# Expert 0 of a fused retention and mixture-of-experts kernel: a joint second layer for 96 early and 224 late places, and a new order of the preparation around it

## The chip, the cores and the metric

The kernel runs on one core of one Trainium2 chip. The metric is the device time of one execution in microseconds (us). The kernel before takes 393.67 us in the median of three runs (392.56, 393.67 and 394.03).

## What is computed

The reference is a retention layer (a linear attention with a decay per head) followed by a mixture of eight experts, in which every token goes to one expert alone:

```python
for t in range(S):                       # B=4, H=8, S=768, D=64
    state = gamma * state + k_t^T v_t
    y[t] = scale * q_t @ state
x = y as (3072 tokens, 512)
logits = x @ w_gate; expert_idx = argmax(logits)
gate_w = softmax(logits)[expert_idx]
for e in range(8):                       # w1: 512 x 1024, w2: 1024 x 512
    h = np.maximum(x[mask_e] @ w1[e], 0)
    out[mask_e] = gate_w[mask_e] * (h @ w2[e])
```

Counted from the reference's own inputs (its seed is 0), expert 0 gets 185 tokens of the first 1536 and 174 of the last 1536; the other seven get 347 to 417.

## The kernel before

**The attention part** works on 24 chunks of 128 tokens, two to a step, k = 0 to 11. A step multiplies scores, carries the state, forms the outputs, turns the tokens' rows (`rows`, L299), computes the gate's logits (`logits` L315, its copy to `LT` at L320, `finish_logits` L322) and, for groups of chunks, ranks the tokens (`gating`, L336). Each chunk's rows are sent to a table in HBM, sorted by expert, by an indirect DMA that GpSimd issues (`send_x`, L306; `SENDS` says which chunks in which step). `after` (L446) holds GpSimd's queue until a value is there.

**Expert 0 is done in two parts.** Its tokens of the first twelve chunks ("early", at most `EARLY` = 224 places) are worked on while the last chunks are still being gated: `early_half` (L698) computes their hidden layer (`hidden`, in halves handed out by `FILL`, with the low parts by `low`) and their output rows (`result`, L722, and `send`, L736). Its other tokens ("late", `CAPS[0]` = 224 places) are position 0 of `moe_main` (L744). The seven other experts follow, sorted by their counts, with `CAPS[1:]` places.

**Precision.** Every product is made of three float32r products of high and low parts: weights are cast on ScalarE into `whi` and the rest subtracted into `wlo` (`split`, L136; 512 or 1024 columns at a time), tokens likewise into `xh` and `xl`, hidden values into `hh` (ScalarE, L897) and `hl` (VectorE, L898). A part of the weights is 1 MB, four parts to an expert; `fetch` (L129) brings one into one of two `raw` buffers, on SyncE's queue. The split weights and other tiles share 11 slots in a pool.

**The first layer** of a position has 8 steps f, each with 12 matmuls into one of three PSUM tiles `ph`, over the position's whole width. **The second layer** has two forms. "Natural" (`natural`, positions 0 and 7): the hidden values are stationary, 128 tokens at a time, the weights move, 24 matmuls of 512 columns for each 128 tokens, and the rows are scaled (`put_rows`, L816) and scattered whole. The other form: a quarter of the weights' columns is stationary, the tokens move, 24 matmuls over the whole width for each of four quarters k; the result in one of two PSUM tiles `py` is transposed on VectorE into `Z` (`turn`, L827), weighted (`weigh`, L833) and scattered in slices of 128 values by GpSimd (`put_slices`, L838), 32 places at a time, during the next position.

**Four widths.** `by_count` (L779) branches on TensorE over four copies of the matmuls: `CAPS[e]`, or 1, 2 or 3 `STEPS` less, by the number that `count_columns` (L776) loads into a register. Position 0 has one width.

**The order is written out by hand** (`manual_schedule`): `jobs` in `moe_main` (L851 to L879) hang the splits, fetches and weightings on the steps f and k. At position 0 the next expert's rows are prepared (`prep_x`, L810: a transpose on VectorE, a cast on ScalarE, a subtraction) at k = 0, three of the four blocks with the subtraction on GpSimd. Parts 0 and 1 of expert 1 are split at f = 2, 3, 5, 6, part 2 at k = 0. In the attention part `SPLITS` (L55) says at which step two quarters of a part of expert 0 are split.

## Time and profile before

| | |
|---|---|
| time, median of three runs | 393.67 us (392.56 to 394.03) |
| the profiled execution: its time, and the span of its instructions | 394.31 us, 392.5 us |
| TensorE (PE) busy | 381.1 us (97% of the span), 3277 matmuls |
| its weight loads (PEld) busy | 354.2 us (90%) |
| VectorE (DVE) busy | 246.6 us (63%) |
| ScalarE (ACT), GpSimd (POOL) busy | 153.4 us (39%), 165.1 us (42%) |
| the chain that ended last, by engine | PE 83%, DMA 7%, issue 4%, DVE 2% |
| granted TensorE clock | 0.997 |

A row of a timeline gives start, duration, engine, line, operation, the names of what is written and read, the shape, and in brackets the idle time of the engine before it with what ended that. PE is TensorE, PEld its weight loads, DVE VectorE, ACT ScalarE, POOL GpSimd, SPq the DMA queue of SyncE. A row of the chain gives start, duration and what ran, with the count of instructions. Attention takes the span up to about 103 us, mixed with the start of expert 0; the rest is experts.

### The profile page before, as it was taken

How to read it: one execution, taken by the hardware profiler on the slowest of the kernel's cores; microseconds unless marked ns; L12 is line 12 of the kernel's file. 1: busy time of each engine (PE TensorE's matmuls, PEld its weight loads, DVE VectorE, ACT ScalarE, POOL GpSimd, SP SyncE). 2: the span in 40 equal slices, each digit the busy share in tenths (PEclk: the TensorE clock that was granted, in tenths of full speed). 3: DMA queues.
4: the chain of work that ended last, by engine and by line, in shares of the span. 5: the costliest groups of instructions: out<-in, count | busy, mean ns of one | idle time of the engine just before them, and what ended most of it. 6: DMA issues, size and time to landing. Idle time of an engine off the chain costs nothing.

```text
span 392.5 us, 8600 instructions
## 1 busy us (share of the span) xinstructions
PE 381.1 (97%) x3277; PEld 354.2 (90%) x3277; DVE 246.6 (63%) x475; ACT 153.4 (39%) x308; POOL 165.1 (42%) x153
## 2 busy tenths in 40 slices
PE   7998999999899999999999999999999999999993
PEld 4787889888798979999999999999999999999972
DVE  4548756795795766773966387477738657666220
ACT  2335435553641545531552354054334415423100
POOL 0333646676751040000485078218506822841552
PEclk9999999999999999999999999999999999999998
DMA  7998899997348778375356557825844773530111
GB/s 276 404 359 315 319 410 384 383 362 253 131 134 236 245 200 254 132 186 143 130 161 202 142 175 244 210 97 168 230 136 152 253 187 137 179 123 10 43 56 50
DMA packets 29821, 80.57 MB, mean 205 GB/s; under 512 B 4556, under 2 KB 18384, under 8 KB 23348
## 3 DMA queue, kind: packets, MB, share of 16 engines
q1 hardware_dynamic: 24740, 66.80, 52.2%
q0 software_dynamic: 5008, 12.69, 8.7%
q8 instruction: 58, 0.95, 1.0%
q14 instruction: 15, 0.12, 0.1%
HBM read 65.00 MB, written 15.08 MB: 204 GB/s over the span
## 4 chain that ended last, share of the span: by engine, by line
PE 83%; DMA 7%; issue 4%; DVE 2%; SPq 2%; POOL 1%; ACT 0%; POOLq 0%; DVEq 0%
PE ph L888 33%; PE py L922 27%; PE py L920 6%; PE Y L287 3%; DMA qkv_t<-qkv 3%; DMA raw<-w 3%; PE sp L246 3%; PE py L729 3%; PE ph L712 3%; PE xp L302 2%; PE U L260 2%; PE Y L276 1%; DMA xn<-xs_dram 1%; PE L L318 1%; SPq L225 1%
## 5 line engine op out<-in xcount | busy, mean ns | idle before, releaser
L670 POOL DMA_INDIRECT out<-Z,sidx x80 | 93.9, 1173 | 136.8 <-DVE Z L836 99.9
L142 DVE TENSOR_TENSOR wlo<-raw,whi 128x1024 fp32r<-128x1024 f32 (+1 forms) x66 | 76.6, 1164 | 12.1 <-ACT whi L141 11.2
L141 ACT CAST whi<-raw 128x1024 fp32r<-128x1024 f32 (+1 forms) x72 | 67.5, 951 | 4.0 <-DMA raw<-w 3.9
L897 ACT ACTIVATE hh<-ph 128x224 fp32r<-128x224 f32 (+7 forms) x64 | 31.2, 489 | 94.5 <-PE ph L888 81.8
L922 PE MATMUL py<-hh,whi 128*128 128x392 f32 (+4 forms) x192 | 66.0, 344 | 0.0
L922 PE MATMUL py<-hl,whi 128*128 128x392 f32 (+4 forms) x192 | 65.9, 343 | 0.0
L922 PE MATMUL py<-hh,wlo 128*128 128x392 f32 (+4 forms) x192 | 65.7, 342 | 0.0
L898 DVE SCALAR_TENSOR_TENSOR hl<-ph,hh 128x224 fp32r<-128x224 f32 (+7 forms) x64 | 35.2, 551 | 35.0 <-ACT hh L897 30.2
L888 PE MATMUL ph<-xh,wlo 128*128 128x392 f32 (+5 forms) x224 | 49.1, 341 | 0.0
L888 PE MATMUL ph<-xh,whi 128*128 128x392 f32 (+5 forms) x224 | 48.9, 340 | 0.0
L888 PE MATMUL ph<-xl,whi 128*128 128x392 f32 (+5 forms) x224 | 48.8, 339 | 0.0
L888 PEld LDWEIGHTS ph<-xl,whi 128*128 128x128 f32 x224 | 40.3, 188 | 0.2
L888 PEld LDWEIGHTS ph<-xh,whi 128*128 128x128 f32 x224 | 40.2, 188 | 0.3
L888 PEld LDWEIGHTS ph<-xh,wlo 128*128 128x128 f32 x224 | 40.3, 188 | 0.2
L689 ACT CAST xh<-xt 128x512 fp32r<-128x512 f32 (+7 forms) x26 | 14.4, 555 | 57.4 <-DVE xt L680 52.0
L922 PEld LDWEIGHTS py<-hh,wlo 128*128 128x128 f32 x192 | 36.1, 188 | 0.2
L922 PEld LDWEIGHTS py<-hl,whi 128*128 128x128 f32 x192 | 36.0, 188 | 0.2
L922 PEld LDWEIGHTS py<-hh,whi 128*128 128x128 f32 x192 | 36.0, 188 | 0.1
L235 POOL TENSOR_TENSOR vs<-qkv_t,cs 128x512 f32<-128x512 f32 x19 | 19.8, 1041 | 38.1 <-DMA qkv_t<-qkv 31.0
L249 DVE TENSOR_TENSOR Sb<-sp,xgs 128x512 f32<-128x512 f32 x48 | 29.8, 682 | 4.4 <-PE sp L246 4.4
L831 DVE STREAM_TRANSPOSE Z<-py 128x416 f32<-128x416 f32 (+3 forms) x24 | 15.0, 626 | 24.6 <-PE py L922 22.9
L265 ACT ACTIVATE ub<-U,cs 128x64 f32<-128x64 f32 x80 | 18.6, 315 | 26.1 <-PE U L260 25.7
(141 smaller groups left out, 523.1 us busy)
## 6 DMA issues: line engine op xcount, KB each, us to landing
raw<-w SPq DMA_DIRECT2D x32, 1024.0 KB
qkv_t<-qkv SPq DMA_DIRECT2D x18, 1024.0 KB
qkv_t<-qkv SPq DMA_DIRECT2D x4, 768.0 KB
xgs<-xs_dram SPq DMA_DIRECT2D x12, 211.2 KB
qkv_t<-qkv SPq DMA_DIRECT2D x4, 512.0 KB
xgs<-xs_dram SPq DMA_DIRECT2D x8, 195.0 KB
out<-Z,sidx POOLq DMA_INDIRECT x80
xs_dram<-zero SPq DMA_DIRECT2D x6, 195.0 KB
```

Of the source, the lines that this page charges most:

```text
L141: nc.scalar.copy(out=hi[:, h], in_=raw[:, h])
L142: engine.tensor_tensor(out=lo[:, h], in0=raw[:, h], in1=hi[:, h].bitcast(F32), op=ALU.subtract)
L235: engine.tensor_tensor(out=vs, in0=qs[g][:, 2].rearrange("a (h d) -> a h d", d=D), in1=cv[:, c, :].unsqueeze(2).broadcast_to([P, H, D]), o ...
L249: nc.vector.tensor_tensor(out=Sb[:, r], in0=sps[r], in1=M[:, r], op=ALU.mult)
L265: nc.scalar.activation(out=ubs[g % 3][:, p], in_=U[:, p], func=AF.Copy, scale=k_("ratio")[:, at:at + 1])
L670: sc = tc.nc.gpsimd.indirect_dma_start(out=out, out_offset=bass.IndirectOffsetOnAxis(ap=index, axis=0), in_=rows, in_offset=None, bounds_c ...
L831: nc.vector.transpose(out=Zs[e][:, 0:nb, k, :], in_=py[:, 0:32 * nb].rearrange("p (j c) -> p j c", c=32))
L888: nc.tensor.matmul(out=ph[:, :w], lhsT=wparts[e, f // 4][a][:, kd, fo:fo + P], rhs=x[:, kd, :w], start=(n == 0), stop=(n == 3 * KD - 1))
L897: nc.scalar.activation(out=hh[:, :cap], in_=ph[:, :cap], func=AF.Relu)
L898: nc.vector.scalar_tensor_tensor(out=hl[:, :cap], in0=ph[:, :cap], scalar=0.0, in1=hh[:, :cap].bitcast(F32), op0=ALU.max, op1=ALU.subtract)
L920: nc.tensor.matmul(out=py[:w, :], lhsT=x[:, k * P:k * P + w], rhs=a[:, f % 4, :], **se)
L922: nc.tensor.matmul(out=py[:, :cols], lhsT=a[:, f % 4, k * P:(k + 1) * P], rhs=x[:, :cols], **se)
```

## The change

- **Expert 0's second layer.** Only the first 128 early tokens keep their own second layer (`result(0, ..)`, `send(0)`). The other 96 early places (`REST`) and the 224 late ones get a joint one in the form of experts 1 to 6: four quarters k, 24 matmuls each, in four widths of 320, 304, 288 or 272 columns, 16 apart (`WIDE`, `STEPS`), chosen by the late count. `hh` and `hl` become one ring of 9 each, and the 96 early places are copied into it at f = 1. Ten slices of 32 places are transposed, weighted and scattered; their names and weights are taken by `take_names`.
- **Expert 1's preparation.** Splits: part 0 at f = 2, 3; part 1 at k = 1, 2; part 2 at k = 3. `prep_x` goes to f = 7, k = 0 (two) and k = 1, with the subtraction on VectorE. The fetch of part 3 moves from f = 7 to k = 2.
- **Before position 0.** The rows of the late tokens are prepared ahead of the counts and limits on VectorE; the clearing behind expert 1's rows is issued before its weights.
- **In attention.** `SPLITS` moves a pair of quarters from step 3 to 4 and one from 4 to 5; `SENDS` moves one chunk from step 11 to 10; `FILL` moves half a hidden step behind the last ranking; one `low` goes from GpSimd to VectorE.

```diff
-STEPS = [0, 10, 8, 8, 8, 8, 8, 8]
+REST = EARLY - 128
+WIDE = [REST + EARLY, *CAPS[1:]]
+STEPS = [16, 10, 8, 8, 8, 8, 8, 8]
-FILL = (1, 3, 2, 2)
+FILL = (1, 2, 3, 2)
-SENDS = {4: (0, 1), 5: (1, 3), 6: (3, 5), 7: (5, 7), 8: (7, 10), 9: (10, 12), 10: (12, 15), 11: (15, 18)}
-SPLITS = {3: (0, 1), 4: (2, 3), 7: (4, 5), 8: (6, 7), 9: (8, 9), 10: (10, 11)}
+SENDS = {4: (0, 1), 5: (1, 3), 6: (3, 5), 7: (5, 7), 8: (7, 10), 9: (10, 12), 10: (12, 16), 11: (16, 18)}
+SPLITS = {4: (0, 1), 5: (2, 3), 7: (4, 5), 8: (6, 7), 9: (8, 9), 10: (10, 11)}
...
-        for i, g in enumerate(range(SENDS[NCH // 2 - 1][1], GROUPS[-1][0])):
+        for g in range(SENDS[NCH // 2 - 1][1], GROUPS[-1][0]):
             send_x(g)
-            if i == 1:
-                lows(1, nc.gpsimd)
...
-        load_meta(meta8, E, 2)
+        end_of = lambda i: nc.sync.value_load(end7[0:1, i - 1:i], min_val=0, max_val=(E9 + 1) * N)
+        clear(bass.ds(end_of(1), ZROWS))
         number = lambda i: nc.sync.value_load(eid7[0:1, i - 1:i], min_val=1, max_val=E - 1)
         expert_at[1] = number(1)
         fetch(1, 0)
-        end_of = ...
-        clear(bass.ds(end_of(1), ZROWS))
...
+        lows(KF, nc.vector)
+        token_index(sidx0, meta0, cnt0)
+        xhl1 = new_xhl()
+        ... (turn_slices and cut_slices of xt1, moved up here)
         (limit, fits, spare, far, beyond)
-        lows(KF, nc.vector)
-        token_index(sidx0, meta0, cnt0)
         result(0, 0)
         result(0, 1)
         send(0)
-        ... (turn_slices and cut_slices of xt1)
-        result(1, 0)
-        result(1, 1)
-        send(1)
+        take_names(late_from, xg1)
+        ... (gone0, slices0)
...
             if more:
-                for part, s0, f0 in ((0, 3, 0), (1, 6, 2)) if e else ((0, 2, 4), (1, 5, 7)):
-                    job(f0, fetch, e + 1, part if e else part + 2)
+                if not e:
+                    for i, eng in halves:
+                        job(2 + i, split, 1, 0, i, eng)
+                        job(KF + 1 + i, split, 1, 1, i, eng)
+                        job(KF + 3, split, 1, 2, i, eng)
+                    job(4, fetch, 1, 2)
+                    job(KF + 2, fetch, 1, 3)
+                    for j, f in enumerate((KF - 1, KF, KF, KF + 1)[:nxt]):
+                        job(f, prep_x, 1, j, nc.vector)
...
-                if e == 0 and f < 3:
-                    nc.vector.memset(ph[:, cap:], 0.0)
                 (hh on ScalarE, hl on VectorE)
+                if e == 0 and f < 3:
+                    nc.vector.memset(ph[:, cap:], 0.0)
+                if e == 0 and f == 1:
+                    early = [h[:, :, P:EARLY].bitcast(F32) for h in hhl0]
+                    nc.scalar.copy(out=HH[:, 0:KF, 0:REST], in_=early[0])
+                    nc.vector.tensor_copy(out=HL[:, 0:KF, 0:REST], in_=early[1])
+                if e == 0 and f in (3, 4):
+                    nc.vector.memset(pys[f - 3][:, WIDE[0] - 3 * STEPS[0]:CMAX32], 0.0)
...
-                    prep_x(e + 1, j, nc.gpsimd if not e and j < 3 else nc.vector)
-                if not e and k == 0:
-                    for i, eng in halves:
-                        split(1, 2, i, eng)
+                    prep_x(e + 1, j, nc.vector)
+                for fn, a in jobs[KF + k] if not e else ():
+                    fn(*a)
```

How the order moves is shown at three places. The first is ScalarE from attention step 3 to step 5: `whi` is a cast of expert 0's weights, `xgs<-L` the copy of the logits to `LT`, `xn<-xp` the tokens' rows, `ub` belongs to the state, `ex` to the gate of step 3. Before:

```order
L265 ACTIVATE ub_119<-U,cs 128x64 x4
L141 CAST whi<-raw 128x512 x2
L320 COPY xgs<-L 128x256
L304 COPY xn<-xp 128x4x128 x2
L265 ACTIVATE ub_120<-U,cs 128x64 x4
L364 ACTIVATE ex<-sh 128x48
L265 ACTIVATE ub_121<-U,cs 128x64 x4
L141 CAST whi<-raw 128x512 x2
L320 COPY xgs<-L 128x256
```

After:

```order
L271 ACTIVATE ub_120<-U,cs 128x64 x4
L326 COPY xgs<-L 128x256
L310 COPY xn<-xp 128x4x128 x2
L271 ACTIVATE ub_121<-U,cs 128x64 x4
L370 ACTIVATE ex<-sh 128x48
L271 ACTIVATE ub_122<-U,cs 128x64 x4
L144 CAST whi<-raw 128x512 x2
L326 COPY xgs<-L 128x256
L310 COPY xn<-xp 128x4x128 x2
L271 ACTIVATE ub_120<-U,cs 128x64 x4
L271 ACTIVATE ub_121<-U,cs 128x64 x4
L144 CAST whi<-raw 128x512 x2
```

In step 3 no cast stands ahead of the copy of the logits any more; steps 4 and 5 have one each.

The second place is VectorE from the last counts to the first `hl` of position 0. `xt` and `xhl` are the late tokens' rows, `xn<-py` the scaled early rows, `limit` to `beyond` the limits. Before:

```order
L621 TENSOR_SCALAR beyond<-far 128x105
L720 TENSOR_TENSOR hl_1618<-rx_1616,hh_1617 128x224 x2
L190 TENSOR_SCALAR far<-cs,cnt_78 128x2
L192 TENSOR_SCALAR ids<-meta_82 128x2
L194 SCALAR_TENSOR_TENSOR sidx_84<-ids,far 128x2
L733 TENSOR_SCALAR xn<-py_2046,meta_82 128x4x4x32
L680 STREAM_TRANSPOSE xt_1827<-xg_1826 128x4x4x32
```

In the changed kernel, after the last subtraction of the late rows:

```order
L703 TENSOR_TENSOR xhl<-xt_1830,xhl 128x4x32
L629 TENSOR_TENSOR se<-sel,cnt 128x49
L630 TENSOR_REDUCE limit<-se 128x7
L631 TENSOR_TENSOR limit<-limit,cs 128x7
L634 TENSOR_TENSOR fits<-cnt,cs 128x3
L635 TENSOR_TENSOR fits<-limit,cs 128x3x7
L638 TENSOR_REDUCE spare<-fits 128x8
L640 TENSOR_TENSOR far<-cs,limit 128x105
L642 TENSOR_SCALAR beyond<-far 128x105
L746 TENSOR_SCALAR xn<-py_2059,meta_82 128x4x4x32
L413 TENSOR_SCALAR slices_84<-xg_1829 128x7
L415 COPY share_86<-xg_1829 128x7
```

The limits stood ahead of the late rows and now stand behind them; behind these rows come three more small instructions (`gone` twice, `slices`) and then the first `hl`.

The third place is VectorE in position 0's second layer: `xt`, `xl` belong to expert 1's rows, `wlo` to its weights, `yo` and `Z` to position 0's results. Before:

```order
L680 STREAM_TRANSPOSE xt<-xgs 128x4x4x32 x3
L680 STREAM_TRANSPOSE xt<-xgs 128x3x4x32
L690 TENSOR_TENSOR xl<-xt,xh 128x4x68
L142 TENSOR_TENSOR wlo<-raw,whi 128x1024 x2
L822 TENSOR_SCALAR yo<-py_2148,meta_83 128x4x4x32
```

After:

```order
L703 TENSOR_TENSOR xl<-xt,xh 128x4x128
L693 STREAM_TRANSPOSE xt<-xgs 128x4x4x32
L703 TENSOR_TENSOR xl<-xt,xh 128x4x128
L842 STREAM_TRANSPOSE Z<-py_2122 128x10x32
L145 TENSOR_TENSOR wlo<-raw,whi 128x1024
L794 UNCONDITIONAL_BRANCH
L693 STREAM_TRANSPOSE xt<-xgs 128x3x4x32
L703 TENSOR_TENSOR xl<-xt,xh 128x4x68
L842 STREAM_TRANSPOSE Z<-py_2123 128x10x32
L794 UNCONDITIONAL_BRANCH x4
L145 TENSOR_TENSOR wlo<-raw,whi 128x1024
L842 STREAM_TRANSPOSE Z<-py_2122 128x10x32
```

Three blocks of expert 1's rows now stand ahead of the first transpose into `Z`, the fourth and a split ahead of the second.

More of the change, by code (lines that the diff above doesn't have):

```diff
@@ L500, in retention_moe @@
             if last:
-                hidden, low, result, send = early_half(tc, ring[:, 4:6].rearrange("a j q m -> a j (q m)")[:, :, 0:DM],
+                hidden, low, result, send, hhl0 = early_half(tc, ring[:, 4:5].rearrange("a j q m -> a j (q m)")[:, :, 0:DM],
                                             wk.tile([P, 4, EARLY], F32, name="rx0", tag="xT"),
@@ L581, in retention_moe @@
             nc.vector.tensor_reduce(out=eid7, in_=se, axis=AX.X, op=ALU.add)
-        for i in (14, 15):
-            split(0, *divmod(i, 4), nc.vector, 1)
         past = gsm.tile([P, E1], F32, name="past")
@@ L626, in retention_moe @@
         send(0)
-        xhl1 = new_xhl()
-        pieces = ((0, P), (4, 64), (6, EARLY - P - 64))
-        for j, w in pieces:
-            turn_slices(nc, xt1, xg1, j, w)
-        for j, w in pieces:
-            cut_slices(nc, nc.vector, xhl1[:, 0], xhl1[:, 1], xt1, j, w)
-        result(1, 0)
-        result(1, 1)
-        send(1)
-        token_index(sidx8, meta8, cnt[:, E:E + 1])
+        take_names(late_from, xg1)
+        for at, first, n, lim in ((0, NJ0 - late_from, late_from, cnt0), (late_from, 0, NJ0, cnt[:, E:E9])):
+            nc.vector.tensor_scalar(out=gone0[:, at:at + n], in0=k_("slot")[:, first:first + n], scalar1=lim,
+                                    scalar2=float(BIG), op0=ALU.is_ge, op1=ALU.mult)
+        nc.vector.tensor_tensor(out=slices0, in0=slices0, in1=gone0, op=ALU.add)
     def overflow():
@@ L651, in clear_behind @@
         nc.sync.dma_start(out=x_rows[bass.ds(end_at[e], ZROWS), :], in_=zero)
-    natural = {0: (sidx8, meta8)}
-    moe_main(tc, wparts, fetch, split, xhl1, xgs, clear_behind, load_x, load_meta, token_index, regions, beyond, limit, spare, natural,
-             overflow, out)
+    moe_main(tc, wparts, fetch, split, xhl1, hhl0, slices0, share0, xgs, clear_behind, load_x, load_meta, token_index,
+             regions, beyond, limit, spare, overflow, out)
     most = nc.values_load(top[0:1, 0:1], min_val=0, max_val=N)
@@ L738, in send, with moe_main @@
         scatter_rows(tc, out, sidx0[:w, j:j + 1], yo[:w, j, :])
-    return hidden, low, result, send
+    return hidden, low, result, send, (hh, hl)
 @with_exitstack
-def moe_main(ctx, tc, wparts, fetch, split, xhl1, xgs, clear_behind, load_x, load_meta, token_index, regions, beyond, limit, spare, natural,
-             overflow, out):
+def moe_main(ctx, tc, wparts, fetch, split, xhl1, hhl0, slices0, share0, xgs, clear_behind, load_x, load_meta, token_index,
+             regions, beyond, limit, spare, overflow, out):
     nc = tc.nc
@@ L758, in moe_main @@
     widths = [[min(P, c - a) for a in range(0, c, P)] for c in CAPS]
-    blocks = [-(-c // 32) for c in CAPS]
+    blocks = [-(-c // 32) for c in WIDE]
     xs = {0: (xhl1[:, 0], xhl1[:, 1])}
@@ L873, in moe_main @@
             if more:
-                for part, s0, f0 in ((0, 3, 0), (1, 6, 2)) if e else ((0, 2, 4), (1, 5, 7)):
-                    job(f0, fetch, e + 1, part if e else part + 2)
+                if not e:
[7 more added lines that the diff above has]
+                        job(f, prep_x, 1, j, nc.vector)
+                for part, s0, f0 in ((0, 3, 0), (1, 6, 2)) if e else ():
+                    job(f0, fetch, e + 1, part)
                     for i, eng in halves:
@@ L939, in moe_main @@
                     fetch(e + 1, 3)
[L940 removed]
+                for fn, a in jobs[KF + k] if e else ():
                     fn(*a)
```

86 lines of the change are left out of this document (53 added, 33 removed).

## The prediction

> **What bounds the kernel now.** I read the stretches first (engines busy in a piece of the span), then the chain that ended last. The columns of a stretch are its bounds and length, the busy time of PE, PEld, DVE, ACT and POOL with their instructions, clock, DMA share and GB/s:
>
> ```profile
> 91.60:96.90 5.30, 5.30 (x94) 4.43 (x94) 3.20 (x7) 1.30 (x5) 2.48 (x5) 1.00 0.71 211
> ...
> 112.60:118.30 5.70, 5.70 (x28) 4.62 (x27) 4.39 (x18) 0.81 (x3) 1.73 (x4) 1.00 0.52 101
> ...
> 134.50:145.70 11.20, 11.20 (x51) 8.45 (x51) 8.47 (x12) 4.97 (x8) 3.84 (x3) 1.00 0.71 222
> 145.70:182.50 36.80, 36.80 (x194) 36.10 (x193) 22.99 (x38) 14.10 (x20) 1.92 (x2) 1.00 0.70 199
> 182.50:381.00 198.50, 198.50 (x1106) 195.94 (x1105) 124.28 (x198) 73.58 (x108) 93.87 (x80) 1.00 0.49 150
> ```
>
> In each of the stretches from 112.6 on TensorE is busy for the whole length, and the chain, which names its matmuls by stage (start, length, count), has no gap in between. So a matmul taken out after 112.6 is worth its full time, unless the change makes TensorE wait:
>
> ```profile
> 91.68 0.34 SPq L177
> ...
> 92.58 3.62 DMA xn<-xs_dram
> ...
> 112.86 11.12 PE py L729 x48
> 123.98 10.71 PE ph L888 x96
> 134.69 11.13 PE py L920 x48
> 145.83 18.40 PE ph L888 x96
> 164.23 18.40 PE py L922 x96
> ...
> 271.22 17.20 PE py L922 x96
> ```
>
> The first two rows are the load of expert 0's early rows; the next three are expert 0: early output rows (two blocks, 512 columns), late first layer (224 columns), late output rows (two blocks, 512). Expert 1 follows (422 columns); the last row is expert 5's second layer (392 columns).
>
> **The matmuls.** Removed are 24 of the 48 of L729 and all 48 of L920: 11.12/2 + 11.13 = 16.69 us. Added are 4 x 24 = 96. The late count is 174 (counted from the reference's inputs), not above 224 - 3 x 16 = 176, so the branch takes 272 columns. No row has 272. The nearest on both sides are 224 columns, 10.71/96 = 0.1116 us each, and 392, 17.20/96 = 0.1792 us; on the line between them 272 columns cost 0.1116 + 48 x 0.000402 = 0.1309 us. So the 96 take 12.57 us and the change saves **4.12 us**. Bounds: all as cheap as at 224 columns gives 5.97; the widest of the four (320 columns, 0.1502 us) gives 2.27.
>
> The Trainium skill ("TensorE: Matmul & The Clock Gate", section "Wait — 56ns, not 53.3ns?") gives columns divided by 2.4 GHz plus about 2.5 ns. By it 512 columns cost 0.2158 us where the trace has 0.2317, and the saving would be an estimated 4.4 us; the trace decides.
>
> **What TensorE may newly wait for.** First, position 0 now starts when the first early block is done (118.4 on this trace's scale), 5.56 us sooner, and its rows must be there. The rows that make them, and what stands around them on VectorE:
>
> ```profile
> 113.09 2.02 SPq L177 DMA_DIRECT2D xg<-xs_dram  x4
> 114.88 0.21 DVE L610 TENSOR_TENSOR se<-sel,cnt 128x49 f32<-128x49 f32 x1
> 116.18 0.22 DVE L621 TENSOR_SCALAR beyond<-far 128x105 int32<-128x105 f32 x1
> 118.47 0.75 DVE L733 TENSOR_SCALAR xn<-py,meta 128x512 f32<-128x512 f32 x1 [1.07 <-PE py L729]
> 119.14 1.22 DVE L680 STREAM_TRANSPOSE xt<-xg 128x512 f32<-128x512 f32 x3
> 119.88 1.13 ACT L689 CAST xhl<-xt 128x512 fp32r<-128x512 f32 x3 [6.15 <-DVE xt L680]
> 120.60 1.23 DVE L690 TENSOR_TENSOR xhl<-xt,xhl 128x512 fp32r<-128x512 f32 x3 [0.24 <-ACT xhl L689]
> ...
> L898 DVE SCALAR_TENSOR_TENSOR hl<-ph,hh 128x224 fp32r<-128x224 f32 x8 | 3.0, 386 | 1.3 <-ACT hh L897 0.8 <-issue 0.4
> L894 DVE MEMSET ph<- 128x228 f32 x3 | 0.7, 248 | 0.7 <-PE ph L888 0.6 <-issue 0.2
> ```
>
> From the first transpose to the last cast is 119.88 + 1.13 - 119.14 = 1.87 us, to the last subtraction 2.69. Ahead of them VectorE loses the limits (114.88 to 116.40), so it reaches them near 115.8. When their load landed, no row says; the load of the early rows, of the same size, took from 91.68 to 92.58 + 3.62 = 96.20, 4.52 us, at a DMA share of 0.71. From 113.09 that would be 117.6. Here the share is 0.52, and the last sends, behind which the load waits, lose a `low` of GpSimd ahead of them; I take 115.8 and keep 117.6 as the bound. The rows are then cast by 117.7 and subtracted by 118.5: in time.
>
> Behind them VectorE has the limits (1.5 us and one small instruction more, 1.75), the scaled rows (0.75) and five small ones near 0.2: the first `hl` runs at 122.0 to 122.4, the clearing of its bank to 122.65. TensorE wants that bank again at the fourth step, 118.4 + 3 x 10.71/8 = 122.4: a wait of **0.2**. Then come `hl` and a clearing for two more banks and the copy of 768 early columns (no row shows it; between 0.4 and 0.9, as 1024 columns subtract in 1.22 below); the fifth and sixth steps find their banks free. With the load at 117.6 TensorE would start 1.1 late and wait 0.9 at the fourth step.
>
> Second, expert 1's rows stand ahead of the first transpose that frees a result bank. One block's work shows in expert 1's own second layer:
>
> ```profile
> 166.93 0.70 DVE L680 STREAM_TRANSPOSE xt<-xgs 128x512 f32<-128x512 f32 x1
> 168.32 0.69 DVE L690 TENSOR_TENSOR xl<-xt,xh 128x512 fp32r<-128x512 f32 x1 [0.69 <-ACT xh L689]
> 168.93 0.68 DVE L831 STREAM_TRANSPOSE Z<-py 128x480 f32<-128x480 f32 x1
> ...
> L142 DVE TENSOR_TENSOR wlo<-raw,whi 128x1024 fp32r<-128x1024 f32 x18 | 21.9, 1220 | 3.6 <-ACT whi L141 3.6
> ```
>
> A block takes 168.93 - 166.93 = 2.0 us, since VectorE waits for the cast in the middle. On the old scale the first layer ends at 129.3, the last `hl` 0.9 later; three blocks end at 136.2, the transpose of 320 columns (0.5, from 0.68 for 480) at 136.7. TensorE has done k = 0 and 1 at 129.3 + 2 x 3.14 = 135.6 and wants that bank: a wait of **1.1**. The second transpose comes after a split (1.2) and the short block (1.5), at 139.9, when k = 2 ends: nothing more. Expert 1 starts near 143.0 instead of 145.8, and its rows are ready at 139.4. Bounds: 0 if VectorE gets through the blocks faster, 2.5 if it comes a microsecond later.
>
> Third, weights. The fetch of expert 1's last part now waits on SyncE for a split that VectorE makes at 141.0; queued behind it on SyncE are the clearing, expert 2's rows and its weights. Their rows before, and the one cast that shows a landing behind such rows:
>
> ```profile
> 122.47 1.94 SPq L177 DMA_DIRECT2D xgs<-xs_dram  x4
> ...
> 137.25 0.37 SPq L651 DMA_DIRECT2D xs_dram<-zero  x1
> 142.71 1.91 SPq L177 DMA_DIRECT2D xgs<-xs_dram  x4
> 145.21 0.35 SPq L133 DMA_DIRECT2D raw<-w  x1
> ...
> 132.82 1.05 ACT L141 CAST whi<-raw 128x1024 fp32r<-128x1024 f32 x1 [0.41 <-DMA raw<-w]
> ```
>
> From clearing to rows is 5.46 us, from rows to the cast of the weights behind them 132.82 - 122.47 = 10.35. So expert 2's first weights land at 141.4 + 5.5 + 10.35 = 157.2, while ScalarE asks for them after expert 1's fourth step, 143.0 + 4 x 18.40/8 + 0.7 = 152.9. ScalarE stands still meanwhile, and the hidden values of the fifth step behind it come at 158.3, their low part at 159.4; TensorE wants that bank at the eighth step, 143.0 + 7 x 2.30 = 159.1: **0.3**, between 0 and 2. The ten scatters and three weightings added to expert 1's time lie beside its matmuls: POOL is busy 1.92 of 36.8 us there, DVE 22.99.
>
> **Attention.** In step 3 a cast of weights stands in ScalarE's queue ahead of the copy of the logits:
>
> ```profile
> 33.73 1.14 ACT L141 CAST whi<-raw 128x512 fp32r<-128x512 f32 x2 [2.79 <-DMA raw<-w]
> 34.78 0.36 ACT L320 COPY xgs<-L 128x256 f32<-128x256 f32 x1
> 35.19 0.44 PE L328 MATMUL lp<-cs,xgs 128*128 128x128 f32 x2 [1.06 <-ACT xgs L320]
> ```
>
> The cast waits 2.79 us for its DMA, the logits' copy behind it is late, TensorE stands 1.06 us. With the pair moved the weights are there before step 4. I take **1.1 us**, carried through to the end of attention because all that feeds the end of attention starts from there; bounds 0 (the later loads from HBM don't come sooner) and 1.5 (the subtraction that leaves step 3 delays other work too). One send of a chunk (128 rows of 520 words, 266 KB) now falls into the load of the early rows that starts at 91.6; the stretch moves 211 GB/s, so it costs between 0 and 1.26. I take **0.4**: the stretch's DMA is busy 0.71 only.
>
> The rest costs nothing: `FILL` only exchanges matmuls that TensorE does anyway, the splits of steps 4 and 5 find their weights landed, and the clearing that goes ahead of expert 1's weights on SyncE delays them by its own 0.37 us, 5 us before they are split.
>
> **Sum.** -1.1 + 0.4 - 4.1 + 0.2 + 1.1 + 0.3 = -3.2. The profiled execution, 394.31, would be 391.1. It lies 0.64 above the median of 393.67, so the prediction for a median is **390.5 us**.
>
> **The rivals.** Two of them rest on rows of the page (DMA share in tenths over 40 slices of 9.8 us; a queue's packets, MB and share):
>
> ```profile
> DMA  7998899997348778375356557825844773530111
> ...
> q8 instruction: 58, 0.95, 1.0%
> ```
>
> *VectorE keeps up* (k = 2 finds its bank free, no wait at the fourth step or in expert 1): 390.5 - 1.6 = 388.9. For: it has 13.8 idle us in the stretch of expert 1; against: each block shows its 0.69 us wait for the cast. *VectorE is later still*: the late rows land at 117.6 (2.0 us of waits instead of 0.2), 392.3. For: the one row of a like load; against: the quieter stretch. *Attention gives nothing*: if HBM loads set its pace (the first nine slices show 7 to 9 tenths and more), 1.1 falls away: 391.6. *Expert 2's weights come too late*: from a landing at 156.9 on, each microsecond holds TensorE one; from 160.4 the gain is gone, from 162.4 the kernel is slower by over the bound below. For: the fetch of part 3, the clearing, the rows and the weights are one chain on SyncE; against: it would take a split on VectorE that is 5 us later than worked out. Price at 162.5: 395.8. *Code*: the second layer gets four branches over four copies. The page counts 58 instruction packets with 1.0% of the span of 16 engines, 392.5 x 16 x 0.01/58 = 1.08 us each. If each of the four branches waits for one, 4.3 us: 394.8; for two, 399. Against it: expert 1's 8 first-layer branches and 4 second-layer branches cost nothing (18.40/96 = 0.1917 us a matmul in both). The Trainium skill ("Runtime: NRT & Kernel Launch", "Instruction fetch mechanics") says that a taken branch out of the window of two pages stalls the engine for a DMA fetch; the trace shows no such stall in expert 1.
>
> **Chances.** A measurement of this kernel tells about 0.5%, 2 us, from no change: faster is below 391.7, slower above 395.6. Forecast 0.48 (alone 389.3 to 391.9), VectorE keeps up 0.14, later still 0.18, attention nothing 0.11, weights late 0.05, code 0.04. Faster: 0.45 of the forecast, 0.14, 0.06 of attention = 0.65. Slower: 0.04 of the weights and 0.02 of the code = 0.06. The rest, 0.29, is no change. The range 388.5 to 393.8 holds the first four cases, each with about a microsecond for the unknown prices, and leaves out the last two and the ends of the bounds.
>
> **What would show it.** Right: 24 matmuls of 512 columns, then 96 of 224, then 96 of 272 at 0.13 us; a wait at `py` of the third quarter named after `Z` of about 1 us; `lp` of step 3 without its 1.06. Wrong: the branch on another width; idle of TensorE over 3 us between 112 and 160; a wait of ScalarE for `raw` in expert 1 that reaches TensorE; the early rows landing no sooner than 96.

## The result and the profile after

The changed kernel took **396.52 us** in the median of 16 runs (394.25 to 400.83), the kernel before 393.94 beside it: ratio 1.0062, 95% interval 1.0041 to 1.0083. Faster was forecast, by 3.2 us; by the medians it is slower by 2.6. Beside other kernels on another chip of the same kind the same file took 392.43 against 392.61: 1.0006 (0.9983 to 1.0030). So the forecast gain is missing on both chips, and on the first a further loss is added. Comparisons leave out runs that lay more than 1.5% above a kernel's fastest; where too few were left, no ratio is given; and four of the profiles below (rows_ahead, scalar_shift, attention_alone, low_between) are of such longer runs, so that single waits are read in them and not their times.

The profiled execution took 397.91 us, span 396.1 (394.31 and 392.5 before). Its stretches from the late first layer of expert 0 on, with the columns of the prediction:

```profile
118.55:129.80 11.25, 11.25 (x98) 11.10 (x99) 9.38 (x32) 5.22 (x11) 1.00 (x1) 1.00 1.08 280
129.80:143.93 14.13, 12.53 (x97) 12.10 (x96) 11.11 (x16) 6.43 (x9) 0.00 (x0) 1.00 0.39 119
143.90:183.60 39.70, 38.03 (x194) 35.84 (x193) 23.72 (x41) 13.91 (x20) 10.13 (x10) 1.00 0.67 193
183.60:384.60 201.00, 199.36 (x1107) 195.51 (x1105) 124.40 (x198) 73.57 (x108) 92.81 (x80) 1.00 0.51 154
```

TensorE is no longer busy for the whole of any stretch but the first. Who it waited for from 90 us on (total, times, longest; before, this list ended with the logits and one cast):

```profile
PE py L954 <- issue: 1.5, 2, 1.0
PE py L954 <- DVE Z L842: 1.5, 1, 1.5
PE L L324 <- DVE rk L384: 0.9, 1, 0.9
PE ph L912 <- issue: 0.8, 2, 0.6
PE py L954 <- DVE hl L924: 0.7, 1, 0.7
PE ph L725 <- issue: 0.5, 1, 0.5
PE ph L912 <- ACT xhl L702: 0.4, 1, 0.4
PE py L954 <- ACT hh L923: 0.3, 1, 0.3
```

"Issue" is time in which the engine waited for nothing that the profile shows; among these waits it is new. The chain:

```profile
118.55 11.22 PE ph L912 x96
...
136.49 0.52 DVE Z L842
137.00 0.64 issue
137.64 6.29 PE py L954 x48
143.93 4.59 PE ph L912 x24
...
160.02 5.64 another core or an unknown queue
...
169.55 14.08 PE py L954 x72
183.63 18.26 PE ph L912 x96
...
259.57 0.16 issue
...
281.65 0.52 issue
...
340.90 3.95 PE py L954 x24
344.85 0.95 issue
345.80 12.09 PE py L954 x72
357.89 15.47 PE ph L912 x96
373.36 11.18 PE py L952 x48
```

Expert 1 starts at 143.93 (145.83 before: 1.9 won), expert 2 at 183.63 (182.63: 2.9 lost in expert 1), TensorE ends at 384.54 (380.98: 2.6 more lost in experts 2 to 7). Of these 2.6 us 1.4 are expert 4's (35.72 us instead of 34.30, with the waits of 0.16 and 0.52 above) and 1.1 expert 6's (32.73 instead of 31.65, with that of 0.95). In expert 1 it is ScalarE that stands (casts `whi` of expert 2's weights, hidden values `hh`):

```profile
157.66 1.05 ACT L144 CAST whi<-raw 128x1024 fp32r<-128x1024 f32 x1 [3.99 <-DMA raw<-w]
158.61 0.54 ACT L923 ACTIVATE hh<-ph 128x452 fp32r<-128x452 f32 x1
159.05 1.04 ACT L144 CAST whi<-raw 128x1024 fp32r<-128x1024 f32 x1
160.00 0.55 ACT L923 ACTIVATE hh<-ph 128x452 fp32r<-128x452 f32 x1
165.69 0.55 ACT L923 ACTIVATE hh<-ph 128x452 fp32r<-128x452 f32 x1 [5.14 <-remote]
```

The 3.99 were forecast (4.3). The 5.14 were not: the seventh step's last matmul ended at 159.94 and its `hh` began 5.7 us later. "Remote" says that the profile knows no releaser. I call this a late release.

### The profile page after: what moved, and what is told of

Its sections match the earlier page's. It is cut to its first block, busy times and chain, and to the rows that moved or that the text cites. A ratio compares the mean times of both kernels' runs of the same rounds, so it can differ in the third digit from the quotient of the medians.

```text
span 396.1 us, 8692 instructions
## 1 busy us (share of the span) xinstructions
PE 381.1 (96%) x3301; PEld 353.9 (89%) x3301; DVE 251.4 (63%) x490; ACT 154.3 (39%) x309; POOL 165.6 (42%) x156
## 4 chain that ended last, share of the span: by engine, by line
PE 71%; DMA 10%; DVE 6%; issue 5%; POOL 3%; ACT 2%; another core or an unknown queue 1%; SPq 1%; POOLq 0%; DVEq 0%; ACTq 0%
PE ph L912 30%; PE py L954 27%; DMA qkv_t<-qkv 4%; PE py L952 3%; PE Y L293 3%; PE sp L252 2%; DMA raw<-w 2%; DMA xs_dram<-xn,KEY 2%; PE ph L725 2%; PE xp L308 2%; DMA xn<-xs_dram 1%; POOL xs_dram L683 1%; PE U L266 1%; PE Y L282 1%
## 5 line engine op out<-in xcount | busy, mean ns | idle before, releaser
L683 POOL DMA_INDIRECT out<-Z,sidx x80 | 92.8, 1160 | 124.7 <-DVE Z L847 103.1
L954 PE MATMUL py<-hh,whi 128*128 128x392 f32 (+5 forms) x224 | 75.8, 338 | 3.4 <-issue 1.5
L954 PE MATMUL py<-hl,whi 128*128 128x392 f32 (+5 forms) x224 | 75.2, 336 | 0.7 <-DVE hl L924 0.7
L954 PE MATMUL py<-hh,wlo 128*128 128x392 f32 (+5 forms) x224 | 75.0, 335 | 0.0
L924 DVE SCALAR_TENSOR_TENSOR hl<-ph,hh 128x224 fp32r<-128x224 f32 (+7 forms) x64 | 35.2, 550 | 37.3 <-ACT hh L923 32.4
L954 PEld LDWEIGHTS py<-hh,whi 128*128 128x128 f32 x224 | 42.1, 188 | 5.5 <-issue 3.1
L954 PEld LDWEIGHTS py<-hl,whi 128*128 128x128 f32 x224 | 42.1, 188 | 1.6 <-DVE hl L924 1.4
L954 PEld LDWEIGHTS py<-hh,wlo 128*128 128x128 f32 x224 | 42.1, 188 | 0.2
L842 DVE STREAM_TRANSPOSE Z<-py 128x416 f32<-128x416 f32 (+4 forms) x28 | 17.0, 609 | 24.5 <-PE py L954 21.4
```

The lines of the kernel that those rows point to most:

```text
L683: sc = tc.nc.gpsimd.indirect_dma_start(out=out, out_offset=bass.IndirectOffsetOnAxis(ap=index, axis=0), in_=rows, in_offset=None, bounds_c ...
L842: nc.vector.transpose(out=Zs[e][:, 0:nb, k, :], in_=py[:, 0:32 * nb].rearrange("p (j c) -> p j c", c=32))
L924: nc.vector.scalar_tensor_tensor(out=hl[:, sl], in0=ph[:, :cap], scalar=0.0, in1=hh[:, sl].bitcast(F32), op0=ALU.max, op1=ALU.subtract)
L954: nc.tensor.matmul(out=py[:, :cols], lhsT=a[:, f % 4, k * P:(k + 1) * P], rhs=x[:, :cols], **se)
```

## Theories

Four explanations were tried. **W**: the late weights of expert 2 cause all of expert 1's loss. **I**: ScalarE's own instructions stand at a fixed place of its code. **S**: indirect transfers that GpSimd issues in a row, 1.28 us apart, make releases late. **C**: TensorE's instructions, which the four branches in four widths lengthen, come late.

## Experiments: weights, ScalarE's code, attention

All ratios are to before on the same chip; medians and counts of runs with them.

**rows_ahead** moves two lines:

```diff
+                    job(KF - 1, fetch_x, 2)
-            if more and e:
+            if more and e > 1:
                 job(0, fetch_x, e + 1)
```

> After, with one edit: SyncE clears behind expert 2's rows and loads them in expert 0's eighth step (before the fetch of expert 1's last weights, for which SyncE stands still until 141), not behind that fetch. Expert 2's first weights then have only one split of VectorE ahead of them and should land near 151 instead of 157.2. Theory W (the loss of expert 1 comes from ScalarE standing before expert 2's weights): the wait of 4.0 us for raw and the one of 5.1 us behind it both go, expert 1 takes 36.4 us instead of 39.7, expert 2 starts near 180.3 instead of 183.6, and the time is 3.3 us below after: ratio to before 0.998. Theory I (the 5.1 us are ScalarE's own instruction stream, which stands at a place of the code whatever the weights do): the wait for raw goes, the 5.1 us stay in expert 1's sixth to eighth step, TensorE still waits 1 to 2 us there, and 1.5 us at most are won: ratio 1.002 or above.

Measured: no wait for `raw` is left in expert 1, and expert 1 takes 36.7 us (from its first matmul to expert 2's) instead of 39.7, as W has it. But expert 2 took 41.7 us instead of 36.4, with late releases of its own, and the time was 401.40 (6 runs), 1.0134 (1.0081 to 1.0187). W holds for expert 1 and says nothing on the rest.

**scalar_shift** adds eight copies `nc.scalar.copy(out=top, in_=run[:, 0:1])` at the start.

> After, with eight one-column copies more on ScalarE at the program's start, where it has nothing to do. Theory I: if ScalarE's 5.1 us in expert 1 stand at a fixed number of its instructions, they come eight instructions earlier, in the stretch where it waits 4.0 us for expert 2's weights anyway; the hidden values of the seventh step then come near 160.6 instead of 165.7, TensorE's waits of 0.7 to 1.0 in the second layer go, and the time is 2 to 3 us below after: ratio to before 0.999 to 1.001. Theory W or any other that hangs on transfers or on TensorE: nothing moves, ratio 1.005 to 1.007.

Measured: the standstill stayed at the same step (5.03 us, before the seventh step's `hh`, 6.7 us behind its matmuls); 402.25 (6 runs), 1.0157 (1.0102 to 1.0212). Theory I falls for ScalarE.

**attention_alone** puts `SPLITS`, `SENDS`, `FILL` and the order of two sends into before:

```diff
-FILL = (1, 3, 2, 2)
+FILL = (1, 2, 3, 2)
...
-SPLITS = {3: (0, 1), 4: (2, 3), 7: (4, 5), 8: (6, 7), 9: (8, 9), 10: (10, 11)}
+SPLITS = {4: (0, 1), 5: (2, 3), 7: (4, 5), 8: (6, 7), 9: (8, 9), 10: (10, 11)}
...
+                send_x(sends.pop(0))
                 for j, w in HALVES:
-                    send_x(sends.pop(0))
```

> Before, with the tables of the attention part alone: splits of the first two weights a pair later, four sends in step 10 and two in step 11, FILL 1, 2, 3, 2. By the profile of after the early rows land 1.7 us sooner and the last logits begin 1.5 us sooner. If this is carried to the end (theory of the prediction), the time is 0.7 to 1.5 us below before: ratio 0.996 to 0.998, and the early result (48 matmuls of 512 columns) starts near 111.4 instead of 112.9. Rival: in after the early hidden layer gave 0.9 of it back in a gap of TensorE at 108; if that gap belongs to the attention tables (their FILL and sends), it is seen here too, the early result starts near 112.2, and the ratio is 0.998 to 1.0.

Measured: the last logits began at 99.67 (100.74 before) and expert 1's first step ended at 147.3 (148.1), and no gap near 108. The time could not tell: 395.93 (12 runs), 1.0025 (0.9984 to 1.0065), with six runs from 392.9 to 394.0 and six from 397.9 to 402.3. Its profile shows late releases in experts 2 and 3, without any of the change's edits to the experts' part.

## Experiments: code

**one_width** (on the same chip as these three) has no branch in expert 0's second layer:

```diff
+                elif e == 0:
+                    second_layer(WIDE[0] - 3 * STEPS[0])
```

> After, with the four widths of expert 0's second layer cut to the one that runs (272 columns, no branch; it holds for up to 176 late places, so it leaves out the three wider forms). The matmuls that run are the same. Theory W: nothing changes but the branches' own time, ratio to before 1.005 to 1.007, and the standstill of ScalarE in expert 1 stays. Theory I (code that the branches add shifts what TensorE and ScalarE fetch, and the stalls at branches of experts 1, 4 and 6, 4 us of weight-load gaps in the profile of after, come from that): those gaps and the 5.1 us of ScalarE go or move, ratio 0.993 to 0.999.

Measured: the gap before the second quarter (0.4 in after) was gone, but ahead of the third the weight loads now stood for 2.5 us, until the transpose, which ended at 140.15, TensorE going on at 140.21; the late release in expert 1 was there. Experts 4 and 6 lost nothing at the places named above, but expert 6's first layer lost 1.5 us. 404.29 (6 runs), no ratio. Not decided: one wait hid behind another.

**turn_first** is paced_all (below) with the blocks of expert 1's rows later, so that the transposes come first:

```diff
-                    for j, f in enumerate((KF - 1, KF, KF, KF + 1)[:nxt]):
+                    for j, f in enumerate((KF - 1, KF, KF + 1, KF + 2)[:nxt]):
```

> The kernel paced_all with the third and fourth block of expert 1's rows a quarter later, behind the transposes of the first two quarters of expert 0's second layer. In paced_all TensorE waits there twice for these transposes, 1.2 and 1.6 us by its gaps. Theory of the prediction (VectorE's blocks ahead of the transpose): both waits go, expert 1 starts near 142.4 instead of 145.2, and the time is 2.5 to 3 us below paced_all: ratio to before 0.990 to 0.994. Rival (VectorE is full there, the wait only moves): the waits come back at the last quarter or at expert 1's start, less than 1 us is won, ratio 0.996 to 1.0.

Measured: neither case. The transpose ended at 132.18, 1.4 us ahead of TensorE's need, and TensorE went on at 135.56; expert 1 started 27.6 us behind expert 0's late first layer (25.4 in after). Not all of that is waiting. The second layer's stretch:

```profile
126.67:143.33 16.66, 14.24 (x98) 13.49 (x97) 11.09 (x16) 6.43 (x9) 0.00 (x0) 0.90 0.82 229
```

The granted clock, the third number from the end, was 0.90 on the average of these 16.66 us, which is an estimated 1.7 us of slower matmuls (the last section comes back to it). 394.80 (12 runs), 1.0048 (1.0022 to 1.0073).

**row_again** is turn_first with expert 0's scatters in one row again:

```diff
-                if more:
+                if more and e > 1:
                     for j in range(nb):
```

> The kernel turn_first, with expert 0's ten scatters in one row again (weighed in three groups, as in after), the other experts' still spread. Theory S: hidden values of expert 1's last three steps come 1 to 6 us late, TensorE waits in its second layer, and the time is 1 to 4 us above turn_first, with a wider spread. If the row alone is harmless and only the late weights made it dear, it is as turn_first within 0.5 us.

Measured: 393.45 (12 runs), 1.0019 (0.9996 to 1.0042). No profile of that chip has a late release, so it says nothing on S. But its trace shows best what TensorE waits for:

```profile
132.69 0.40 PE L963 MATMUL py<-hh,whi 128*128 128x272 f32 x1 [0.40 <-issue]
...
134.02 0.51 DVE L844 STREAM_TRANSPOSE Z<-py 128x320 f32<-128x320 f32 x1
...
137.42 0.39 PE L963 MATMUL py<-hh,whi 128*128 128x272 f32 x1 [1.45 <-issue]
```

The transpose that frees the bank ended at 134.53; the third quarter began 2.9 us later, after a wait of 1.45 us for which the profile names no releaser. The packets of q8, the DMA queue that brings instructions, tell the rest. How many there were between 126 and 144 us, in after and then in before (packets, MB, share):

```profile
q8 instruction: 4, 0.07, 1.4%
```

```profile
q8 instruction: 1, 0.02, 0.4%
```

I put the waits beside the packets' own times (worked out from the starts and lengths in the traces). In nine profiles with four widths TensorE's weight loads stood 22 times for over 0.25 us ahead of a second, third or fourth quarter; 21 times they went on 1.67 to 1.73 us after the end of such a packet, and once 1.58. The two other profiles with four widths, paced and scalar_shift, have one such wait each, ahead of the third quarter, and it ended 0.05 us behind the transpose. In after both come together: the transpose ended at 136.99, a packet at 135.97, and the third quarter began at 137.64. Of the 1.5 us that the list above puts down to `Z`, the first 0.8 would have been waited for the transpose in any case, and the last 0.65, the "issue" row of the chain, ended with the code.

**two_widths** and **one_width_first** are turn_first with less code:

```diff
+        if e == 0:
+            with tc.If(fewer[e] < 3) as wide:
+                products(WIDE[e])
+            with wide.Else():
+                products(WIDE[e] - 3 * STEPS[e])
+            return
```

> The kernel turn_first with two widths (320 and 272 columns) and one branch a quarter in expert 0's second layer, in place of four widths and two branches. Theory C (code): in turn_first the first two transposes were done 3.4 us before TensorE began the third quarter, so what it waited for there (2.1 us), and before the second and the fourth (0.8 and 0.6), was its instructions; in seven kernels it goes on 1.7 us after an instruction packet has ended. With half the code most of the 3.5 us goes: expert 1 starts 27 us or less after expert 0's late first layer in place of 27.6 and the time falls by 1.5 to 3 us, ratio to before 0.992 to 0.998. Rival (the transposes or VectorE's order hold it): the third quarter starts as late as before, ratio as turn_first, 1.002 to 1.007.

> The kernel turn_first with the one width that runs (272 columns, up to 176 late places; it leaves out the wider forms) and no branch in expert 0's second layer. Theory C: no gap of TensorE over 0.3 us in expert 0's second layer at all, expert 1 starts 24.0 to 24.5 us after the late first layer's start (11.2 + 12.6 and small waits) in place of 27.6 in turn_first; the time is 2.5 to 3.5 us below turn_first, ratio 0.989 to 0.996, unless code of later experts stalls in its place. Rival as for two widths: no change.

Measured: 389.67 (6 runs), 0.9948 (0.9930 to 0.9967), and 390.10 (12 runs), 0.9946 (0.9919 to 0.9972). The second layer's stretch in two_widths:

```profile
127.31:139.41 12.10, 12.10 (x99) 12.10 (x97) 8.77 (x15) 5.55 (x9) 0.00 (x0) 1.00 0.82 215
```

TensorE is busy for all of it, 12.1 us instead of 14.1, and expert 1 starts 23.0 us behind the late first layer in both. Halving the code does as much as removing it. turn_first ran on another chip, but after_again (below), on the chip of these two, has waits of 0.6 and 1.4 us there, and two_rows and two_spread (below), with two widths on a third chip, have none. So theory C is shown for expert 0's second layer. two_widths is faster than both kernels (after beside it: 392.43), but besides the two edits it holds those of paced_all, so this gain isn't theirs alone.

Other branches stalled too. Ahead of expert 6's second quarter the weight loads stood for 0.8 to 1.4 us in all eleven profiles with four widths, and went on 1.57 to 1.59 us after a packet. With one width (one_width, one_width_first, on two chips) they stood for 1.4 to 1.5 us in expert 6's first layer instead; with two widths for 0.5 us there in two_rows and in neither of the others, though two_widths has a wait of 1.1 us in expert 1, 1.4 us behind a packet. So in expert 6 the place goes with the code and not with the chip. Ahead of expert 4's third quarter they stood in five of the eleven profiles, for 0.85 us (after) to 1.9, and not in after_again, which is the same file as after; what decides there stays open. before shows no such wait, but attention_alone, which has the branches of before, shows one of 1.8 us in expert 4's first layer, 1.4 us after a packet: old branches can stall as well.

## Experiments: late releases

**low_between** puts GpSimd's `lows(1, nc.gpsimd)` back between the second and third of the last sends:

```diff
             send_x(g)
+            if i == 1:
+                lows(1, nc.gpsimd)
```

> After, with one of the changed places put back: GpSimd makes one low part of the early hidden layer between the second and the third of its last sends, as it did before. Theory S (new): when GpSimd issues more than about five indirect transfers in a row, 1.28 us apart, what releases the other engines reaches them late. In after the six sends from 100.7 to 108.2 are such a row (in before two, a subtraction, four), and TensorE has gaps of 1 us near 108 to 109 there. By S these gaps go, expert 0's late first layer starts near 117.6 instead of 118.6, and the time falls by about 0.9 us: ratio to before 1.002 to 1.005. Rival (the gaps come from the fetch of code or from loads): they stay, ratio as after, 1.004 to 1.008.

Measured: as S has it at that place, no gap near 108, late first layer at 117.98 instead of 118.55; 397.86 (12 runs), 1.0041 (0.9997 to 1.0085). But the six sends in a row are not enough for the gap: all five profiles that have them on chips with late releases show it, and the three on other chips (after_again and both of no_slices) don't. Experts 1 and 2 had late releases (3.9 and 1.7 us at the worst).

**paced** weighs and scatters expert 0's blocks one in a step, in expert 1 alone. **paced_all** spreads the scatters of all experts but the last over the next one's steps, and has rows_ahead and low_between too. The spreading in paced_all:

```diff
+                    for j in range(nb):
+                        t = 1 + 15 * j // nb
+                        f = t if t < KF else KF + (t - KF) // 2
+                        job(f, weigh, e - 1, j, 1)
+                        job(f, put_slices, e - 1, j)
```

> After, with expert 0's ten scatters spread over expert 1's steps: each block is weighed by VectorE alone, in a step of its own, ahead of its scatter, so that GpSimd issues one in 2.3 us instead of ten in a row. The data are the same. Theory S: the 5.1 us of ScalarE in expert 1 go, the seventh step's hidden values come near 160.6, and of expert 1's 39.7 us only the wait for the bank behind expert 2's late weights (0.6 to 1.0) is left: expert 2 starts near 181.0 instead of 183.6, ratio to before 0.998 to 1.002. Theory W (what follows from the late weights): nothing but VectorE's ten small instructions changes, the 5.1 us stay, ratio 1.004 to 1.008.

> After, with the low part back between the sends, SyncE's rows of expert 2 ahead of expert 1's last weights, and the scatters of every expert but the last spread over the next one's steps, each block weighed alone. Theory S: no late releases are left in experts 1 to 6, TensorE runs through from expert 1 on, expert 2 starts near 179.5, and the time is 388.5 to 391.5 us, ratio 0.987 to 0.994, with a spread of 2 us at most. Theory W with rows ahead alone: the row of scatters still disturbs at random, ratio 1.00 or above, spread 5 us and more.

Measured: paced 401.40 (6 runs), 1.0131 (1.0064 to 1.0198): the seventh step's `hh` was 1.6 us late instead of 5.7, but the weights were waited for (5.1 us) and expert 2 was disturbed (3.2). paced_all 395.30 (12 runs), 0.9993 (0.9957 to 1.0029): no late release in experts 1 to 6, the last expert's 3.7 as in the other kernels on that chip, and the spread 4.7 us against 8.2 for before. It missed 388.5 to 391.5: 3.5 us of gaps in expert 0's second layer.

**dose** adds ten scatters of a constant to before, in expert 1's fourth step:

```diff
+        for j in range(10):
+            scatter_rows(tc, aside, aside_at[:, j:j + 1], k_("ident"))
```

> Before, with ten scatters added that the computation does not need: 128 rows of 512 bytes each, from a constant to a place of their own in HBM, all given to GpSimd in expert 1's fourth step, where expert 0's ten stand in after. Nothing waits for them and TensorE's work is the same. Theory S: hidden values of expert 1's steps six to eight come 1 to 6 us late, TensorE waits in its second layer, and the time rises by 1 to 4 us: ratio 1.003 to 1.010. Any theory by weights, code or matmuls: no more than ten small instructions of VectorE beside other work, ratio 0.999 to 1.001.

Measured: 400.76 (6 runs), 1.0109 (1.0036 to 1.0181), but not where S put it: 0.8 us late at expert 1's last step, 3.2 in expert 2, which took 41.7 us. Inconclusive, since attention_alone shows late releases in expert 2 (3.2) without the dose.

**no_slices** leaves out expert 0's ten scatters and with them part of the output; it ran twice, the second time beside after:

```diff
+                    if e > 1:
                         job(KF + j * steps // nb if more else ..., put_slices, e - 1, j)
```

> After without expert 0's ten scatters in expert 1 (it leaves out the writing of expert 0's joint block to the output; all else is as in after, the late weights of expert 2 too). Theory S: ScalarE still waits 4 us for expert 2's weights, but the seventh step's hidden values come near 160.6 instead of 165.7, and TensorE's waits in expert 1's second layer (0.7 to 1.2 each) go: expert 2 starts 2 to 3 us sooner after expert 1's start than in after (39.7 us), so 36.7 to 37.7. Theory W (the standstill follows from the late weights): expert 1 still takes 39 us or more. The time by S is 2 to 3 us below after unless a later expert is disturbed: ratio to before 0.998 to 1.003.

> After itself, unchanged, beside the others of this call on the same chip. Theory S (rows of scatters make releases late): expert 1's seventh step's hidden values are 4 to 7 us behind its matmuls again, expert 1 takes over 38.5 us, ratio 1.004 to 1.009. If late releases belong to some chips or states alone, they can be missing here: then the step is 1 us late, expert 1 takes 37.5 to 38.2 us, and the ratio is 1.000 to 1.003, by the code's and the late weights' part alone.

> The kernel no_slices again (after without expert 0's ten scatters, whose part of the output it leaves out), to stand beside after on the same chip. Theory S: where after shows the seventh step 4 us late or more, this one shows 1.0, and expert 1 is shorter by 1.5 to 3 us. If both show the same, be it 1 or 6, the scatters are not what makes it late.

Measured: 393.30 (12 runs), 1.0018 (0.9993 to 1.0042), and 393.31 (12 runs), 1.0030 (1.0003 to 1.0057); after beside the second 392.43 (12 runs), 1.0006. The seventh step was 1.0 us late in both, 0.1 in after. With all its scatters after shows there, for the same two steps of ScalarE as above:

```profile
155.91 1.05 ACT L144 CAST whi<-raw 128x1024 fp32r<-128x1024 f32 x1 [3.63 <-DMA raw<-w]
156.87 0.54 ACT L923 ACTIVATE hh<-ph 128x452 fp32r<-128x452 f32 x1
157.30 1.04 ACT L144 CAST whi<-raw 128x1024 fp32r<-128x1024 f32 x1
158.24 0.99 ACT L923 ACTIVATE hh<-ph 128x452 fp32r<-128x452 f32 x2
```

The same wait for weights, and nothing late behind it: expert 1 took 37.3 us, 39.7 on the first chip. Late releases belong to some chips or their conditions. The last expert, whose program is the same in all, shows it: there the seventh step was late, by 3.5 to 3.7 us nearly always, in all profiles of before, after and three groups of runs (that of rows_ahead, of low_between and of two_rows), and on time in all of the two other groups (that of no_slices and of two_widths). Each group ran on one chip.

**before_paced** puts the lines that paced_all adds for the scatters into before.

> Before, with its scatters spread over the steps as in the kernel paced_all (each block weighed alone ahead of its scatter) and nothing else. Theory S: rows of scatters disturb experts 2 to 6 of before too, though seldom; spread out, the median falls by 0.3 to 1.5 us and the slowest of the runs by several: ratio 0.996 to 0.999, spread under 3 us. If before is not disturbed by them at all, the ratio is 1.000 to 1.002 (ten instructions more on VectorE in each expert).

Measured: 392.70 (12 runs), 0.9998 (0.9983 to 1.0012): nothing to be won on a chip without late releases.

**two_rows** and **two_spread** (the file of two_widths) differ in the spreading alone; two_rows lacks it:

```diff
                 if more:
-                    for j in range(nb):
...
-                        job(f, put_slices, e - 1, j)
-                elif more:
```

> The kernel two_widths with every expert's scatters in rows again, weighed in groups of four, as in after and before. Theory S: where the profile shows late releases in the last expert (whose scatters stand in a row in all kernels; 3.5 us on some chips, none on others), experts 1 and 2 are disturbed too, and the time is 2 to 6 us above two_spread. On a chip that shows none in the last expert it is as two_spread within 1 us, and the ratio to before is 0.993 to 0.997. If it is as two_spread on a chip with late releases, theory S falls.

> The kernel two_widths once more, on this call's chip, beside the one with rows. Theory C (code) alone gives the same as there: ratio to before 0.992 to 0.998, expert 1's start 23 us behind expert 0's late first layer's. Theory S: no late release in experts 1 to 6 on any chip.

Measured: 389.79 (6 runs), 0.9897 (0.9858 to 0.9936), and 390.91 (6 runs), 0.9920 (0.9894 to 0.9947). This chip has late releases; ScalarE in two_rows' last expert:

```profile
362.34 0.47 ACT L931 ACTIVATE hh<-ph 128x360 fp32r<-128x360 f32 x1 [1.91 <-PE ph L920]
367.34 0.83 ACT L931 ACTIVATE hh<-ph 128x360 fp32r<-128x360 f32 x2 [4.53 <-remote]
```

Yet experts 1 and 2 lost nothing to the rows. Theory S falls in the form that a row alone is enough. What all traces bear out is narrower: on chips with late releases, expert 1's seventh step was 3.9 to 6.7 us late in the four kernels that both keep the row and wait for expert 2's weights at the sixth step, 1.6 in paced, which waits but has part of the row spread, and at most 0.3 in the seven that do not wait there. rows_ahead shows that the wait is needed for it; no run takes away the row and nothing else on such a chip, so that the row is needed too is not shown. Why a release comes late, and why expert 2 was disturbed in some kernels and not in others on such chips, stays open.

## Why the prediction was wrong, point by point

- **Matmuls: right.** 48 of 272 columns took 6.29 us, 0.131 each (0.1309 forecast); the branch took 272 columns. (The row of 392 columns was named expert 5's; it is expert 4's, and expert 5's width is the same.) The Trainium skill's formula ("TensorE: Matmul & The Clock Gate", "Wait — 56ns, not 53.3ns?") would give an estimated 0.116; the measurement decides.
- **First layer of expert 0: right in its waits.** Its load was issued at 111.76, VectorE took the rows up at 116.62; TensorE waited 0.4 at the start and 0.2 at the fourth step (0.2 forecast). It started at 118.55 and not 117.7, since 0.9 us were lost near 108, where the change lets six sends follow one another; with low_between they were not, nor in after_again.
- **Second layer of expert 0: right as far as it went, but one of two waits.** The wait forecast at 1.1 us for VectorE's transpose ahead of the third quarter was there, about 0.8 us in after, under the forecast name `Z`. Behind it 0.65 us more ended with an instruction packet, and 0.4 stood before the second quarter, also behind a packet. The profile's waits add up to 1.9 us in after_again. Either repair alone (turn_first, one_width) brought nothing; with both of them (two_widths, one_width_first) no wait is left.
- **Weights of expert 2: landing right, price wrong.** 157.2 was forecast and measured, the wait 4.3 against 3.99. TensorE's wait for the bank was 1.0 and not 0.3 (VectorE made the weights' low part first). The bound of 2 us was broken on the first chip: with the late release behind it the term cost 2.9; on the other chip 0.5 (37.3 against 36.8). rows_ahead, without the wait, took 36.7 on a chip with late releases.
- **Attention: right.** `L` began 1.5 us sooner; the early rows had landed by 94.5. In attention_alone's one profile 0.8 us of this reached expert 1 (0.7 forecast, 1.1 less 0.4). ScalarE's copy of step 3's logits now waits for TensorE alone:

```profile
32.44 0.37 ACT L326 COPY xgs<-L 128x256 f32<-128x256 f32 x1 [2.30 <-PE L L324]
```

- **The step that failed** is the setting aside of the rival *Code*, which left the sum without a term for it. It was set aside because "expert 1's 8 first-layer branches and 4 second-layer branches cost nothing". The new branches cost what those did not: 0.3 to 2.2 us at a quarter that stalled, where no transpose was waited for. Branches in experts 4 and 6 stalled too, 2.5 us together in after. The Trainium skill ("Runtime: NRT & Kernel Launch", "Instruction fetch mechanics") says that a taken branch out of the two-page window stalls the engine; the traces agree that a fetch ends the stall, with 1.7 us behind the packet as its tail, and no run here shows the window. I weighed this rule by the old branches and gave it 0.04. Why those of expert 1, with as many instructions in less time (2.3 us a step), did not stall stays open.
- **The second failure** is the size of the term for expert 2's weights: 0.3, at most 2, against 2.9 on the first chip. Nothing in the sum allowed for a late release, and why one comes stays open.
- **Where the missing time lies.** The profiled execution's span was forecast at 389.3 us (392.5 - 3.2) and was 396.1. Of the 6.8 us 0.9 lie ahead of the late first layer, 0.8 in expert 0's two layers, 2.6 in expert 1 and 2.6 in experts 2 to 7. On the chip without late releases 3.0 us are missing by the medians (392.61 - 3.2 = 389.4 against 392.43); by the stages of after_again's trace 1.5 lie in expert 0's two layers, 0.2 in expert 1 and 1.3 in experts 2 to 7, nearly all in expert 6. So waits behind instruction packets are about half of what is missing on the first chip and most of it on the other.

## What to carry to other kernels

Code is a resource with a transfer time: a new data-dependent branch with four bodies must be priced by its instruction packets, and old branches that run free are no proof for it; with this late count two bodies gave what four were meant to give. Where two waits end close together, removing one shows the other: test them apart and together before calling either harmless. ScalarE's hidden values stood here behind a cast that waited 4 us for weights of the next expert, and this held up the present one; loads for the next stage belong ahead of such waits (rows_ahead).

## What the hardware showed unasked

After the waits in expert 2 of rows_ahead TensorE ran slower. Its stretches before, just behind a wait of its weight loads of 1.85 us, and later:

```profile
204.00:208.00 4.00, 4.00 (x23) 3.93 (x22) 1.56 (x2) 1.13 (x3) 3.09 (x4) 1.00 0.31 111
216.50:220.50 4.00, 3.96 (x13) 3.81 (x14) 3.31 (x5) 1.57 (x2) 0.00 (x0) 0.57 0.88 167
221.00:225.00 4.00, 4.00 (x23) 3.97 (x22) 2.60 (x6) 0.91 (x2) 0.00 (x0) 1.00 0.85 252
```

The granted clock fell to 0.57 and 13 matmuls were made in the time of 23: by the trace the clock stood at half for 3.4 us, so the wait cost an estimated 1.7 more behind it. The same came behind waits of 2.0 to 3.2 us in turn_first, low_between, dose and scalar_shift (there for 6.8 us), and a second time in rows_ahead. The length of the wait alone does not decide: 2.5 us in one_width and 2.15 in paced had nothing behind them. The other surprise is the chips: one and the same program lost 2.6 us to before on one and nothing on another.
